# Memory recall of a whole segment in sixteen 32 by 32 tiles, with a new written order that puts all of Q ahead of K

## The chip, the cores and the metric

The kernel runs on one core of one Trainium2 chip. A core has five engines that run side by side and wait for each other only through semaphores: TensorE (PE, matrix products, with PEld for its weight loads), VectorE (DVE), ScalarE (ACT), GpSimd (POOL) and SyncE (SP, whose queue here issues nearly all DMA transfers). Working memory is SBUF, 128 partitions; matrix products land in PSUM, 128 partitions in 8 banks of 512 float32 columns each. The metric is the device time of one execution in microseconds (us); the time of a kernel is the median of its runs. A profile is one execution recorded by the hardware; its span is what lies between its first and last instruction.

## The reference

Two branches over the same input x (2048 tokens by 512) are mixed by a gate per token. Branch A is attention in four segments of 512 tokens with a memory that is carried from segment to segment, 32 heads of 16; branch B is a gated feed-forward layer of width 1792.

```python
for s in range(4):                      # segments of 512 tokens
    logits = einsum('bhqd,bhkd->bhqk', qs, ks) * scale + mask
    a_dot = einsum('bhqk,bhkd->bhqd', softmax(logits), vs)
    pq = phi(qs)                        # where(t > 0, t + 1, exp(t))
    num = einsum('bhld,bhde->bhle', pq, M)
    den = einsum('bhld,bhd->bhl', pq, z)[..., None] + 1e-06
    outs.append(g * num / den + (1 - g) * a_dot)     # g = sigmoid(beta), per head
    M = M + einsum('bhld,bhle->bhde', phi(ks), vs)
    z = z + einsum('bhld->bhd', phi(ks))
a = concat(outs) @ wo
gate, up = x @ W_gate, x @ W_up
b = (relu(gate) * up) @ W_down
g = sigmoid((x * gate_w).sum(-1))
return g * a + (1 - g) * b
```

The product of phi(q) with M is the memory recall; segment 0 has no memory, so recall exists for segments 1, 2 and 3.

## The kernel before

The kernel is first recorded as a list of tasks: each `plan.add` names an engine, a planned duration, what it depends on, the buffers it needs and frees, and a function that emits the instructions. The two strings at the top decide the rest: `ORDER` is the order in which all tasks are emitted, and so the order of each engine's queue, and `UNITS` says which buffer of a ring (or which PSUM bank) each task gets. The planned durations no longer act; they are what a planner used when it wrote the order.

The work of a segment, in chunks c of 128 feature columns (8 heads), one unit u for each chunk of each segment:

- **Start.** x of segment 0 is loaded in rows and transposed by TensorE (L483), with some products on constants ahead to keep TensorE at work (`heat`, L883) and a pair on junk after them (L501). wq comes in four transfers split over the SP and ACT queues, wk in two halves, then wv, the weights of branch B in pieces, and wo in one transfer (`load_cols`, L266). x of later segments comes by a transposing DMA (L273), and again in rows as `xn` (L276) for the token gates.
- **Projections.** `proj_q`, `proj_k` and `proj_v` (matmuls through `full`, L446 where the tile is the whole 128 by 128 array, L450 where it is cut into four column tiles of 32). VectorE copies the results out of PSUM (L542 for Q, L558 for K, L588 for V) and masks K into KT (L561); phi of Q and K is formed with an exponential on ScalarE (L520) and two VectorE instructions (L515, L516). phi(K) is transposed by DMA into pK (L574).
- **Attention.** A visit of scores (`qk`, L609; the diagonal, L622) uses row tiles of 32 by 128: four heads at once, each with its own rows of the array and its own bank of the PSUM banks 0 to 3. ScalarE takes the exponential of four banks at once (L631), GpSimd masks (L660), and `pv` multiplies with V in column tiles of 128 by 32 (L682), twice for each unit, r = 0 and 1. In `pv`, head pair j is written to the PSUM partitions 32j to 32j + 31. `normalise` transposes the result (L713), takes the reciprocal (L721), and scales (L718); L694 transposes it into oT.
- **Memory.** `memory` adds phi(K) times V (L787, column tiles); VectorE accumulates it (L801, L803) and spreads it into `mbd` (L812), a block-diagonal 128 by 128 matrix for each chunk with the head gate folded in through `bdg`, and into `zbd` (L807) for the denominators.
- **Denominators.** `dens` (L738) forms den for two chunks at once; VectorE adds 1e-6, takes the reciprocal (L751) and multiplies with the token ratio (L752); SP stores the result to DRAM as `coefs` (L756).
- **Recall.** `recall` runs once for each chunk of segments 1 to 3, twelve times. SP loads the coefficients, broadcast over partitions, into one of two buffers `cdr` (L765); one plain product of mbd with phi(Q) of 512 columns goes into one bank; VectorE multiplies the bank with the coefficients into `omr` (L773), and L698 adds it to oT.
- **Branch B and output.** `ffn_tasks`: gate and up products, ReLU on ScalarE (L832), the product hT on VectorE (L838); `out_tile` accumulates hT times wd and oT times wo in one bank, VectorE scales (L864) and SP stores (L869).

Whenever two neighbours in TensorE's queue have different tile shapes (plain 128 by 128, row tiles, column tiles), the shape changes between them. Tasks marked `flex` (the plain ones) take the column form when they directly follow a column task.

`head_gates` (L370 to L378) makes the head gates from beta once: four copies (L373) of 32 partitions, four more instructions. Its lines and those of the recall are printed below.

Of the kernel before, what the change touches and what calls it, by code (L numbers as in the profile page):

```python
# [12 lines left out]
P = 128  # L13
S = 2048
D = 512
# [77 lines left out]
"""  # L93

UNITS = (
    "4132650714730167121200005110331202243100000100100000030110000020010300003201100380200103a1"
    "1240231302c02092202211d220b011311361127301512110100201010103223003111212000123231201220000"
    "02300001000003100003200000210003130000000010122b2139220c31140005022a1002022d21103116203802"
    "011027111310011002203223320012310222303120232230310220000022001101000032001121000000301020"
    "1200005000030282125223d11042017023c2231022a11192076412332323020303b01001212203031023111020"  # L100
    "033012131112000002300005000002301112000000230010220000470007242203821000154103102276016222"
    "9406d301b5223417c603a322501001110021"
)


class Slot:


    def __init__(self, cands):
        self.cands, self.units, self.left = tuple(cands), (), 0  # L110

    @property
# [16 lines left out]
class Plan:  # L129
# [18 lines left out]
    def run(self):  # L148
# [7 lines left out]
        for s, n in zip(slots.values(), UNITS):  # L156
            s.units = s.cands[int(n, 16)]
# [21 lines left out]
def kernel(  # L179
# [137 lines left out]
    load_gu(2)  # L317
    load_gu(3)
    got_d = [load_wd(0, 7, "d0"), load_wd(7, NF, "d1")]
    got_o = load_cols(nc.sync, wo_sb, A_wo, 0, D, "o")  # L320
    plan.add("SP", 24500, -1e9, None, xfer=5700.0)


# [563 lines left out]
    for seg in range(NSEG):  # L887
# [15 lines left out]
        for c in range(NC):  # L903
            if seg:
                recall(seg, c)
# [41 lines left out]
```

## Time and profile before

| | us |
|---|---|
| median of 3 runs (266.73 to 267.23) | 266.76 |
| the profiled execution, its own time | 266.88 |
| its span | 265.18 |

The span is 1.6 to 1.7 us shorter than the time, since the time also holds what lies around the first and last instruction. Work of the engines by group, with the costliest of each:

| group | instructions | busy us | mean ns |
|---|---|---|---|
| L446 plain products for gate and up | 393 | 106.8 | 380 |
| L631 exponentials of the scores, ScalarE | 64 | 120.2 | 1878 |
| L838 hT, VectorE | 56 | 38.1 | 685 |
| L713 transposition of the attention result, VectorE | 32 | 22.1 | 703 |
| L773 recall times coefficients, VectorE | 12 | 8.2 | 680 |

Reading it: a matmul's duration (380 ns for 512 columns) runs from its start to its last result, and the next one starts before that, so busy time and the distance between starts are two things. "Idle before" an engine's instruction counts only if that engine is on the chain that ends last.

### The profile page before, as it was taken

The page shows a single profiled execution, that of the slowest core. Times are in us where ns is not written, and L with a number is a line of the kernel's source. Part 1 is how long each engine was busy: PE and PEld are TensorE (multiplying, and loading weights), DVE is VectorE, ACT ScalarE, POOL GpSimd, SP SyncE. Part 2 cuts the span into 40 slices and gives each one's busy share as a digit, 9 for nine tenths or more (in the row PEclk, how much of TensorE's full clock was granted, in tenths as well). Part 3 has the DMA queues.
Part 4 walks back from the last instruction along what each step waited for, and adds up shares of the span by engine and source line. Part 5 has one row for each costly group of instructions (what it writes and reads, how often), then busy time and mean ns, then how long its engine had stood idle before and what let it go on. Part 6 is the DMA issues. An engine that isn't in the chain of part 4 may idle for free.

```text
span 265.2 us, 8154 instructions
## 1 busy us (share of the span) xinstructions
PE 257.7 (97%) x3499; PEld 119.7 (45%) x3530; DVE 202.7 (76%) x456; ACT 182.4 (69%) x168; POOL 60.3 (23%) x162
## 2 busy tenths in 40 slices
PE   8999999999999999999999999999999999999995
PEld 5443444444444344444443444444444544444554
DVE  3497797999997897998967779979777537764822
ACT  3189899879877789888686976984886656841100
POOL 7014262303142043112312141131204040220000
PEclk9999999999999999999999999999999999999999
DMA  7999990030064024252000632500110000300011
GB/s 203 305 256 339 285 165 0 9 96 2 2 125 54 0 76 67 62 92 64 0 2 4 90 75 79 114 4 2 55 38 0 22 2 22 109 0 2 2 62 40
DMA packets 29931, 19.41 MB, mean 73 GB/s; under 512 B 14920, under 2 KB 28360, under 8 KB 29896
## 3 DMA queue, kind: packets, MB, share of 16 engines
q1 hardware_dynamic: 29320, 18.38, 29.7%
q8 instruction: 27, 0.44, 0.7%
q10 hardware_dynamic: 576, 0.52, 0.6%
q14 instruction: 8, 0.07, 0.1%
HBM read 13.21 MB, written 2.55 MB: 59 GB/s over the span
## 4 chain that ended last, share of the span: by engine, by line
PE 94%; DMA 3%; issue 1%; DVE 1%; DVEq 0%
PE ps L446 65%; PE ps L450 12%; PE ps L609 8%; PE ps L682 7%; DMA wk_sb<-in_A_wk_dram 2%; DMA xn<-in_A_x_dram 1%; PE ps L622 1%; PE ps L787 1%; DVE T L713 1%; PE ps L738 0%; DVE osr L864 0%; DVEq L713 0%
## 5 line engine op out<-in xcount | busy, mean ns | idle before, releaser
L631 ACT ACTIVATE E<-ps 128x2048 bf16<-128x2048 f32 x64 | 120.2, 1878 | 30.9 <-PE ps L609 29.2
L660 POOL TENSOR_SCALAR_AFFINE_SELECT E<-E 128x256 bf16<-128x256 bf16 x128 | 52.4, 441 | 171.8 <-ACT E L631 171.8
L838 DVE TENSOR_TENSOR hT<-ps,rgr 128x512 bf16<-128x512 f32 x56 | 38.1, 685 | 23.4 <-PE ps L446 15.8
L446 PE MATMUL ps<-xT,wg_sb 128*128 128x512 bf16 x203 | 55.5, 379 | 0.5 <-issue 0.2
L446 PE MATMUL ps<-xT,wu_sb 128*128 128x512 bf16 x190 | 51.3, 380 | 1.1 <-issue 1.0
L832 ACT ACTIVATE rgr<-ps 128x512 bf16<-128x512 f32 x56 | 32.3, 598 | 19.2 <-PE ps L446 19.0
L446 PE MATMUL ps<-wd_sb,hT 128*128 128x512 bf16 (+1 forms) x163 | 38.6, 352 | 0.6 <-issue 0.5
L446 PEld LDWEIGHTS <-wg_sb 128*128 128x128 bf16 x208 | 19.4, 98 | 23.7 <-issue 2.1
L446 PEld LDWEIGHTS <-wu_sb 128*128 128x128 bf16 x202 | 18.1, 98 | 22.7 <-issue 3.4
L609 PE MATMUL ps<-QT,KT 32*128 32x320 bf16 (+3 forms) x512 | 25.4, 273 | 0.0
L713 DVE STREAM_TRANSPOSE T<-ps 128x512 f32<-128x512 f32 x32 | 22.1, 703 | 4.0 <-PE ps L682 3.7
L446 PEld LDWEIGHTS <-hT 128*128 128x128 bf16 x167 | 14.4, 98 | 16.0 <-issue 2.1
L864 DVE TENSOR_SCALAR osr<-ps,ngcol 128x512 bf16<-128x512 f32 (+2 forms) x18 | 12.3, 687 | 10.2 <-PE ps L450 6.1
L682 PE MATMUL ps<-E,Vp 128*17 128x320 bf16 (+3 forms) x512 | 19.2, 273 | 0.5 <-DVE T L713 0.4
L450 PE MATMUL ps<-wd_sb,hT 128*32 128x512 bf16 (+1 forms) x340 | 19.4, 362 | 0.0
L609 PEld LDWEIGHTS <-KT 32*128 32x128 bf16 x512 | 7.6, 92 | 25.3 <-issue 25.0
L446 PE MATMUL ps<-xT,wq_sb 128*128 128x512 bf16 (+1 forms) x70 | 17.8, 360 | 0.2 <-issue 0.2
L631 ACT ACTIVATE Em<-ps 128x2048 bf16<-128x2048 f32 x8 | 15.0, 1877 | 4.2 <-PE ps L622 4.2
L446 PE MATMUL ps<-xT,wk_sb 128*128 128x512 bf16 x54 | 15.1, 380 | 0.5 <-DMA wk_sb<-in_A_wk_dram 0.2
L558 DVE CAST ktr<-ps 128x512 bf16<-128x512 f32 x16 | 10.9, 686 | 4.8 <-PE ps L446 4.6
L446 PE MATMUL ps<-wv_sb,xT 128*128 128x512 bf16 x46 | 13.2, 380 | 0.3 <-issue 0.2
L446 PE MATMUL ps<-wo_sb,oT 128*128 128x512 bf16 (+1 forms) x54 | 13.2, 356 | 0.1
(97 smaller groups left out, 284.9 us busy)
## 6 DMA issues: line engine op xcount, KB each, us to landing
cdr<-coefs SPq DMA_DIRECT2D x12, 256.0 KB
out_dram<-osr SPq DMA_DIRECT2D x15, 128.0 KB
wd_sb<-in_B_W_down_dram SPq DMA_DIRECT2D x2, 896.0 KB
xn<-in_A_x_dram SPq DMA_DIRECT2D x3, 512.0 KB
wg_sb<-in_B_W_gate_dram SPq DMA_DIRECT2D x2, 512.0 KB
wu_sb<-in_B_W_up_dram SPq DMA_DIRECT2D x2, 512.0 KB
wg_sb<-in_B_W_gate_dram SPq DMA_DIRECT2D x2, 384.0 KB
wu_sb<-in_B_W_up_dram SPq DMA_DIRECT2D x2, 384.0 KB
```

What stands on the lines that cost most here:

```text
L446: nc.tensor.matmul(out, lhsT=lhsT, rhs=rhs, start=start, stop=stop)
L450: nc.tensor.matmul(out[r], lhsT=lhsT[:, r], rhs=rhs, start=start, stop=stop, tile_position=(0, 32 * j))
L558: d = plan.add("DVE", 600, key - RQK, lambda: nc.vector.tensor_copy(ktr[ks.i][:], bank(sl)), [a], DVL + 40, need=[ks], frees=[sl])
L609: nc.tensor.matmul(ps[:, j * L + o:j * L + o + L - q], lhsT=KT[i][rows, kb, 3 * r:3 * r + 2].rearrange("p h q -> p (h q)"), rhs=QT[i][rows ...
L622: nc.tensor.matmul(ps[:, o:o + HP], lhsT=KT[i][rows, kb, 2:4].rearrange("p h q -> p (h q)"), rhs=QT[i][rows, kb * P:kb * P + HP], start=Tr ...
L631: last_exp[0] = [plan.add("ACT", 66 + 4 * L / 1.2, key, lambda: nc.scalar.activation(dst, ps[:, 0:4 * L], ACT.Exp, scale=SCALE), [a] + war ...
L660: nc.gpsimd.affine_select(out=m[:, :, o:o + HP], in_=m[:, :, o:o + HP], compare_op=ALU.is_ge, fill=0.0, base=HP, pattern=[[0, 4], [1, HP]] ...
L682: nc.tensor.matmul(bank(sl)[32 * j:32 * j + HW, q:q + w], lhsT=(Vp[i] if n < 4 else Vm)[:, kb, r, 4 * c + j, 0:HW], rhs=rhs, start=(n == 0 ...
L713: done.append(plan.add("DVE", 633, key - RL, lambda r=r, sl=sl: nc.vector.transpose(T[ts.i][:, r], bank(sl)), [a] + done, 75 if r else 0, ...
L832: r = plan.add("ACT", 478, key - RL, lambda sl=gsl, rs=rs: nc.scalar.activation(rgr[rs.i][:], bank(sl), ACT.Relu), [g], ACL, frees=[gsl])
L838: nc.vector.tensor_tensor(hT[hs1.i][:], bank(sl), rgr[rs.i][:], ALU.mult)),
L864: nc.vector.tensor_scalar(osr[os.i][:, n0 - c0:n1 - c0], bank(sl)[:, 0:n1 - n0], ngcol[:, tt:tt + 1], None, ALU.mult)),
```

## The change

Five edits belong together, and the order is written anew over all of them (1,339 tasks in place of 1,348).

1. **Recall by segment.** `recall(seg)` is one task for a whole segment: for each chunk c and each head pair j, one product of a 32 by 32 tile, at rows 32j and columns 32m of the array with m = (j - c) mod 4, 16 products of 512 columns. Chunk c still has its own bank, so four banks are held at once; the four tiles of one bank come from four different row groups, and the four tiles of one row group go to four banks. Four VectorE multiplications follow, one for each bank.
2. **Rotated partitions.** So that recall and attention line up, head pair j of chunk c now stands at the PSUM partitions 32m in `pv` too. The rows of `wo` are loaded rotated to match, in seven transfers in place of one, and the head gates are rotated: `head_gates` has 25 small VectorE instructions in place of 8, and the mask `bd` is built with copies on GpSimd.
3. **Smaller memory matrix.** `mbd` keeps only its diagonal blocks, 32 columns for each chunk, so that each of the two spreading instructions writes 128 by 64 elements in place of 128 by 256.
4. **Coefficient buffers.** Chunks 0 and 1 use two fixed buffers `cdr`; chunks 2 and 3 use the space of `xn` once the token gates of that segment are formed. The reload of `xn` for the next segment waits for the recall's multiplications of chunks 2 and 3. `omr` has four buffers in place of three.
5. **A new written order**, made with assumed landing times of wq 0.6 us earlier. At the start TensorE's queue has the products of Q chunks 1, 3, 0 (and half of the last) ahead of the first of K; before, the first halves of three K chunks stood between them, and the pair on junk stood ahead of the first Q and now stands between K products. The transposing load of x for segment 2 now stands on SP right behind the first weights. The head gates stand on VectorE before the first feed-forward products are done, in place of after the first segment's first unit.

```diff
-    got_o = load_cols(nc.sync, wo_sb, A_wo, 0, D, "o")
-    plan.add("SP", 24500, -1e9, None, xfer=5700.0)
+    for c in range(NC):
+        n = P - 32 * c
+        nc.sync.dma_start(out=wo_sb[0:n, c, :], in_=A_wo[(c + 1) * P - n:(c + 1) * P, :])
+        if c:
+            nc.sync.dma_start(out=wo_sb[n:P, c, :], in_=A_wo[c * P:(c + 1) * P - n, :])
+    got_o = arrival("o")
+    plan.add("SP", 27500, -1e9, None, xfer=5700.0)
...
+    def turned(c):
+
+        return [(j, (j - c) % 4) for j in range(4)]
+
     def head_gates():
-        gb = gcat[:, 1]
-        for j in range(4):
-            nc.vector.tensor_copy(ebq[32 * j:32 * j + 32], eb.rearrange(
-                "p (c j r) -> p j c r", j=4, r=2)[32 * j:32 * j + 32, j])
-        nc.vector.tensor_scalar(gb, ebq[:], 1.0, None, ALU.add)
-        nc.vector.reciprocal(gb, gb)
-        nc.vector.tensor_tensor(gcat[:, 0], ebq[:], gb, ALU.mult)
-        nc.vector.tensor_tensor(bdg[:], bd.rearrange("p c (j r) -> p c j r", r=2),
-                                gb[:, :, None, :].to_broadcast([P, NC, 4, 2]), ALU.mult)
+        nc.vector.tensor_scalar(gall[:, 1], eb[:], 1.0, None, ALU.add)
+        nc.vector.reciprocal(gall[:, 1], gall[:, 1])
+        nc.vector.tensor_tensor(gall[:, 0], eb[:], gall[:, 1], ALU.mult)
+        g = gall.rearrange("p k (c j r) -> p k c j r", j=4, r=2)
+        for m in range(4):
+            rows = slice(32 * m, 32 * m + 32)
+            nc.vector.tensor_copy(gcat[rows, 1], g[rows, 1, :, m])
+            for c in range(NC):
+                nc.vector.tensor_copy(gcat[rows, 0, c], g[rows, 0, c, (m + c) % 4])
+        for r, m in enumerate((mcol_e, mcol_o)):
+            nc.vector.tensor_scalar(bdg[:, :, r], gcat[:, 1, :, r], m[:, 0:1], None, ALU.mult)
...
-                    for j in range(4):
+                    for j, m in turned(c):
...
-                            bank(sl)[32 * j:32 * j + HW, q:q + w],
+                            bank(sl)[32 * m:32 * m + HW, q:q + w],
...
-    def recall(seg, c):
...
-        a = plan.add("PE", 216, key, lambda col: full(
-            bank(sl), mbd[i][:, c].rearrange("p j r e -> p (j r e)"), pqT[u % RQ][:], True, True,
-            col), [prj["pq", seg, c], att["mbd", seg - 1], (b, 3900.25)], PEL, need=[sl], flex=1)
...
+    def recall(seg):
+        i, sls = seg % 2, [work() for _ in range(NC)]
...
+        coef = [cdr[0][:], cdr[1][:]] + [xn.bitcast(F32).rearrange(
+            "p (k t) d -> p k (t d)", k=2)[:, k] for k in range(2)]
...
+        def pe():
+            for c in range(NC):
+                for j, m in turned(c):
+                    rows = slice(32 * j, 32 * j + 32)
+                    nc.tensor.matmul(bank(sls[c])[32 * m:32 * m + 32],
+                                     lhsT=mbd[i][rows, c].rearrange("p r e -> p (r e)"),
+                                     rhs=pqT[units[c] % RQ][rows, :], start=True, stop=True,
+                                     tile_position=(32 * j, 32 * m))
+        a = plan.add("PE", 230, key, pe, [prj["pq", seg, c] for c in range(NC)]
+                     + [att["mbd", seg - 1]] + [(b, 3900.25) for b in loads], PEL, need=sls,
+                     mode="quad", size=16)
+        for c, u in enumerate(units):
+            om = plan.one("omr")
+            att["recall", u] = a
+            att["omul", seg, c] = plan.add("DVE", 605, key - RL, lambda c=c, om=om: (
+                nc.vector.tensor_tensor(omr[om.i][:], bank(sls[c]), coef[c], ALU.mult)),
+                [a, loads[c]], DVL, need=[om], frees=[sls[c]])
+            recalled[u] = att["omul", seg, c], om
...
-                    mbd[n][:, :, :, r, :],
-                    mzacc[:, :, r, None, 0:DH].to_broadcast([P, NC, 4, DH]),
-                    bdg[:, :, :, r, None].to_broadcast([P, NC, 4, DH]), ALU.mult)
+                    mbd[n][:, :, r, :], mzacc[:, :, r, 0:DH],
+                    bdg[:, :, r, None].to_broadcast([P, NC, DH]), ALU.mult)
...
             got_n[seg] = [plan.add("SP", 520, KA(4 * seg - 4), lambda seg=seg: load_xn(seg),
-                                   att["xn", seg - 1], 6500, xfer=1700.0)]
+                                   att["xn", seg - 1] + [att[k] for k in (
+                                       ("omul", seg - 1, 2), ("omul", seg - 1, 3)) if k in att],
+                                   6500, xfer=1700.0)]
```

More of the change, by code (lines that the diff above doesn't have):

```diff
@@ L30 @@
 ORDER = """
[62 rows of a table removed]
[62 rows of a table added]
 """
 UNITS = (
[L96 to L102, printed above, removed]
+    "765432100132020000013101220024300002310000001000000012000000000300010000320000101003220101"
+    "1333037221411293125003a1206013d023c0128200b00110010001000003000101111202000012221300456102"
+    "1000000300000002300000000200000000021000212021042231103832220016112b200332370109023d102522"
+    "6c010a100010003030007050103121103020013433212012450011000003200000002300000000210002000001"
+    "00022313012212031271013301542062134310a1029420b0218202c113d1100001030206070303030202331200"
+    "004563201000003200000003200000000010000000760000134203022222121201602230025023a504c3137312"
+    "83119407b625d00110112100"
 )
@@ L156, in run @@
         for s, n in zip(slots.values(), UNITS):
-            s.units = s.cands[int(n, 16)]
+            s.units = s.cands[int(n, 36)]
         for t in self.tasks:
@@ L232 @@
     oT = [sb([P, NC, L], BF16, f"oT{i}") for i in range(2)]
-    mbd = [sb([P, NC, 4, 2, DH], BF16, f"mbd{i}") for i in range(2)]
+    mbd = [sb([P, NC, 2, DH], BF16, f"mbd{i}") for i in range(2)]
     zbd = [sb([P, NC, 4, 8], BF16, f"zbd{i}") for i in range(2)]
@@ L243 @@
     cfr = ring([P, 2, 16], F32, "cfr", 2)
-    omr = ring([P, L], BF16, "omr", 3)
+    omr = ring([P, L], BF16, "omr", 4)
     dnr = ring([P, P], F32, "dnr", 2)
-    cdr = ring([P, L], F32, "cdr", 2)
+    cdr = [sb([P, L], F32, f"cdr{i}") for i in range(2)]
     osr = ring([P, D], BF16, "osr", 3)
@@ L255, in work @@
         return plan.one("ps", range(7, -1, -1))
-    LANDS = dict(n0=3600, n1=3800, n2=4300, n3=4450, qa=5700, qb=6450, ka=7250, kb=8550, v=10050,
+    LANDS = dict(n0=3600, n1=3800, n2=4300, n3=4450, qa=5100, qb=5900, ka=7250, kb=8550, v=10050,
                  g0=11550, u0=13000, gw=14400, be=14650, g1=15900, u1=17250, x1=20700, g2=22000,
-                 u2=23100, g3=24200, u3=25300, d0=28100, d1=30800, o=32100)
+                 u2=23100, g3=24200, u3=25300, d0=28100, d1=30800, o=33600)
     def arrival(name):
@@ L334 @@
     bd = sb([P, NC, 8], F32, "bd")
-    nc.gpsimd.memset(bd[:], 1.0)
-    nc.gpsimd.affine_select(out=bd[:], in_=bd[:], compare_op=ALU.is_ge, fill=0.0, base=0,
-                            pattern=[[0, NC], [-16, 8]], channel_multiplier=1)
-    nc.gpsimd.affine_select(out=bd[:], in_=bd[:], compare_op=ALU.is_ge, fill=0.0, base=15,
-                            pattern=[[0, NC], [16, 8]], channel_multiplier=-1)
-    bdg = sb([P, NC, 4, 2], F32, "bdg")
+    bdg = sb([P, NC, 2], F32, "bdg")
     tri = sb([P, P // 2], BF16, "tri")
@@ L350 @@
         nc.gpsimd.memset(zbd[i][:], 0.0)
+    nc.gpsimd.memset(bd[:, 0], 1.0)
+    nc.gpsimd.affine_select(out=bd[:, 0], in_=bd[:, 0], compare_op=ALU.is_ge, fill=0.0, base=0,
+                            pattern=[[-16, 8]], channel_multiplier=1)
+    nc.gpsimd.affine_select(out=bd[:, 0], in_=bd[:, 0], compare_op=ALU.is_ge, fill=0.0, base=15,
+                            pattern=[[16, 8]], channel_multiplier=-1)
+    for g in range(1, NC):
+        nc.gpsimd.tensor_copy(bd[:, g, 0:8 - 2 * g], bd[:, 0, 2 * g:8])
+        nc.gpsimd.tensor_copy(bd[:, g, 8 - 2 * g:8], bd[:, 0, 0:2 * g])
     eb = sb([P, H], F32, "eb")
-    ebq = sb([P, NC, 2], F32, "ebq")
+    gall = sb([P, 2, H], F32, "gall")
     gcat = sb([P, 2, NC, 2], F32, "gcat")
@@ L368 @@
     nc.gpsimd.memset(rcol[:], 0.0)
+    def turned(c):
+        return [(j, (j - c) % 4) for j in range(4)]
     def head_gates():
-        gb = gcat[:, 1]
-        for j in range(4):
-            nc.vector.tensor_copy(ebq[32 * j:32 * j + 32], eb.rearrange(
-                "p (c j r) -> p j c r", j=4, r=2)[32 * j:32 * j + 32, j])
-        nc.vector.tensor_scalar(gb, ebq[:], 1.0, None, ALU.add)
-        nc.vector.reciprocal(gb, gb)
-        nc.vector.tensor_tensor(gcat[:, 0], ebq[:], gb, ALU.mult)
-        nc.vector.tensor_tensor(bdg[:], bd.rearrange("p c (j r) -> p c j r", r=2),
-                                gb[:, :, None, :].to_broadcast([P, NC, 4, 2]), ALU.mult)
+        nc.vector.tensor_scalar(gall[:, 1], eb[:], 1.0, None, ALU.add)
[9 more added lines that the diff above has]
+            nc.vector.tensor_scalar(bdg[:, :, r], gcat[:, 1, :, r], m[:, 0:1], None, ALU.mult)
     got_eb = plan.add("ACT", 200, 0.0, lambda: nc.scalar.activation(
         eb[:], betab[:], ACT.Exp, scale=-1.0), [got_be], 100)
-    got_gates = plan.add("DVE", 1400, 0.0, head_gates, [got_eb], 100, lock=True)
+    got_gates = plan.add("DVE", 2000, 0.0, head_gates, [got_eb], 100, lock=True)
     PEL, DVL, ACL, POL = 230, 150, 165, 130
@@ L682, in pv @@
                         nc.tensor.matmul(
-                            bank(sl)[32 * j:32 * j + HW, q:q + w],
+                            bank(sl)[32 * m:32 * m + HW, q:q + w],
                             lhsT=(Vp[i] if n < 4 else Vm)[:, kb, r, 4 * c + j, 0:HW],
-                            rhs=rhs, start=(n == 0), stop=(n == 7), tile_position=(0, 32 * j))
+                            rhs=rhs, start=(n == 0), stop=(n == 7), tile_position=(0, 32 * m))
             a = plan.add("PE", 550, key - PVP + r, pv, masks + [prj["v", seg, t] for t in range(4)]
@@ L758, in dens @@
             xfer=700.0)
-    def recall(seg, c):
-        i, u, sl = seg % 2, 4 * seg + c, work()
-        key = KA(u - LEAD, -4000)
-        cs, om = plan.one("cdr"), plan.one("omr")
-        n, k = 2 * seg + c // 2, c % 2
-        b = plan.add("SP", 620, key - 3000, lambda: nc.sync.dma_start(
-            out=cdr[cs.i][:], in_=coefs[n][8 * k:8 * k + 8].rearrange("h t p -> h (t p)")[:, None]
-            .to_broadcast([8, 16, L])), [att["coefs", seg, c // 2]], 4200, need=[cs],
-            xfer=1850.0)
-        a = plan.add("PE", 216, key, lambda col: full(
-            bank(sl), mbd[i][:, c].rearrange("p j r e -> p (j r e)"), pqT[u % RQ][:], True, True,
-            col), [prj["pq", seg, c], att["mbd", seg - 1], (b, 3900.25)], PEL, need=[sl], flex=1)
-        att["recall", u] = a
-        a = plan.add("DVE", 605, key - RL, lambda: nc.vector.tensor_tensor(
-            omr[om.i][:], bank(sl), cdr[cs.i][:], ALU.mult), [a, b], DVL, need=[om],
-            frees=[sl, cs])
-        recalled[u] = a, om
+    def recall(seg):
+        i, sls = seg % 2, [work() for _ in range(NC)]
+        key = KA(4 * seg - LEAD, -4000)
+        units = [4 * seg + c for c in range(NC)]
+        coef = [cdr[0][:], cdr[1][:]] + [xn.bitcast(F32).rearrange(
+            "p (k t) d -> p k (t d)", k=2)[:, k] for k in range(2)]
+        loads = []
+        for c in range(NC):
+            n, k = 2 * seg + c // 2, c % 2
+            war = att["xn", seg] if c > 1 else [att.get(("omul", seg - 1, c))]
+            loads.append(plan.add("SP", 620, key - 3000, lambda c=c, n=n, k=k: nc.sync.dma_start(
+                out=coef[c], in_=coefs[n][8 * k:8 * k + 8].rearrange("h t p -> h (t p)")[:, None]
+                .to_broadcast([8, 16, L])), [att["coefs", seg, c // 2]] + war, 4200, xfer=1850.0))
+        def pe():
+            for c in range(NC):
+                for j, m in turned(c):
[14 more added lines that the diff above has]
+            recalled[u] = att["omul", seg, c], om
@@ L819, in memory @@
         a = plan.add("DVE", 290, key, total, [a], 40, frees=[sl])
-        att["mbd", seg] = plan.add("DVE", 900, key, spread, [a] + war, DVL, lock=True)
+        att["mbd", seg] = plan.add("DVE", 620, key, spread, [a] + war, DVL, lock=True)
     def ffn_tasks(seg):
@@ L903 @@
         for c in range(NC):
-            if seg:
-                recall(seg, c)
+            if seg and c == 0:
+                recall(seg)
             attention(seg, c)
```

124 rows, old and new, of the table ORDER are left out of this document.

## The prediction

> **What bounds the kernel now.** I read the first page, then the chain of waits in order of time, then the costliest groups with shapes kept apart, then the stretches of the first 60 us. The page's first part has TensorE busy nearly throughout (the granted clock is 1.00 in the stretches shown further down):
>
> ```profile
> PE 257.7 (97%) x3499; PEld 119.7 (45%) x3530; DVE 202.7 (76%) x456; ACT 182.4 (69%) x168; POOL 60.3 (23%) x162
> ```
>
> The chain in order of time (start, length, what) gives the two prices on which the sum rests:
>
> ```profile
> 72.48 2.70 PE ps L446 x12
> ...
> 124.39 0.73 DVE T L713
> ...
> 139.39 0.73 DVE T L713
> ...
> 144.69 3.13 PE ps L446 x14
> ```
>
> Stretches of 12 and 14 plain matmuls last 2.70 and 3.13 us, so one more costs 0.215, and 2.70 - 12 x 0.215 leaves 0.12 at the end of a stretch: the drain when the tile shape changes. And only in two places does the chain leave TensorE after the start: the second attention-times-V product (L682) of a unit waits for the transposition (L713) of the first, because the old order gives both the same PSUM bank. The timeline of TensorE shows what that costs:
>
> ```profile
> 124.51 0.60 PE L450 MATMUL ps<-xT,wk_sb 128*32 128x512 bf16 x8
> 125.16 0.62 PE L682 MATMUL ps<-E,Vp 128*17 128x448 bf16 x16
> ...
> 138.73 1.04 PE L450 MATMUL ps<-wd_sb,hT 128*32 128x512 bf16 x16
> 140.16 0.62 PE L682 MATMUL ps<-E,Vp 128*17 128x448 bf16 x16 [0.40 <-DVE T L713]
> ```
>
> Column tiles run four at a time, so 8 of them end 2 x 0.215 after their start: the next could begin at 124.94 and begins at 125.16; 16 of them leave it at 139.59 against 140.16. Together 0.79 us. All other waits of TensorE after the first scores (15.6 us) are under 0.1. So time follows the matmuls, the changes of shape, and those waits.
>
> **The change, part by part.** The sum is made against the profiled execution's span, 265.18; the median shown, 266.76, lies 1.58 above it.
>
> *Recall.* Removed are 12 products of 0.215 (10 plain, as the first row has them, and two as four column tiles, L450):
>
> ```profile
> L446 PE MATMUL ps<-pqT,mbd 128*128 128x512 bf16 x10 | 3.8, 381 | 0.1
> ...
> L787 PE MATMUL ps<-Vp,pK 128*32 128x34 bf16 x192 | 2.0, 183 | 0.0
> ```
>
> That is -2.58. Added are three groups of 16 tiles, 32 by 32, 512 columns each. No row shows 16 at once. Floor: all together, 0.215. Ceiling: the four of a bank one after another, 0.86. Nearest are the rows of four tiles, which do overlap, so I take full overlap plus issue: the update of the memory issues 64 small matmuls in 0.70 us, one lasting 0.183 (L787), so 0.52/63 = 8 ns a step; 15 x 8 ns + 0.215 = 0.34. Three: +1.02.
>
> [...]
>
> *Changes of shape.* Counting along both written orders, matmuls change between plain, row, column and 32 by 32 tiles 146 times before and 151 times after: six for entering and leaving the three groups, one fewer elsewhere. 5 x 0.12 = +0.60, bounds 0.5 to 0.7.
>
> *The two waits.* In the new order no unit's two products share a bank (before: those two units). -0.79; at worst the wait comes back elsewhere, 0.
>
> *New small waits.* I take +0.5, bounds 0 to 1.3. After the third recall VectorE must do four products with the coefficients, two transpositions, three additions and the rest before the last output tiles may start; adding these up, it reaches the third addition about 0.2 after TensorE asks. And the head gates: 8 small VectorE instructions become 25, moved from 36 us to about 18 us. Nearest to a copy of theirs are a small MEMSET and the old copies (starts, and the time from first to last):
>
> ```profile
> 1.08 0.35 DVE L332 MEMSET mcol_e<- 16x1 f32 x4
> ```
>
> ```profile
> L373 DVE COPY ebq<-eb x4: 152/162/371, 35.8 to 36.3; 32x8 f32<-32x8 f32 x4
> ...
> ```
>
> The old ones took 1.7 us. Twenty copies at 0.09 (L332, 0.35 for four) to 0.17 (L373, three steps from 35.8 to 36.3) and 0.9 for the other five make 2.7 to 4.3. Queued behind are a ReLU-gated product hT and the next bank's release; by my addition TensorE asks for that bank 0.4 to 0.5 us after VectorE has it at the lower price, and waits 1.0 at the upper. I take 0.3. Later VectorE gets 1.2 back (six L812 of 0.45 shrink fourfold in width; L749 at 128x128 lasts 0.288), but that is covered.
>
> *Start.* All of Q ahead of K removes the gap at 7.93, but the second half of wk lands only at 9.19:
>
> ```profile
> 7.93 0.98 PEld L446 LDWEIGHTS <-wk_sb 128*128 128x128 bf16 x6 [0.53 <-DMA wk_sb<-in_A_wk_dram]
> 9.19 0.57 PEld L446 LDWEIGHTS <-wk_sb 128*128 128x128 bf16 x4 [0.29 <-DMA wk_sb<-in_A_wk_dram]
> ```
>
> The old order has three first halves of K to do meanwhile; the new one runs three Qs to about 8.6 (its first ones still at the slow pitch of the cold start), one first half to 9.0, then waits, and the keep-warm pair sits in the hole before the first score. Same total work, same holes: 0, bounds -0.4 to +0.4. The first score moves from 15.6 to some 11.5, which only shifts work that TensorE does anyway.
>
> *DMA.* wo comes in seven transfers instead of one; at 0.5 us each on SP (its other loads) that is 1 us more than its 2.44, ahead of the second xT, xn and three pK on the same queue. Before, the xT issue holds SP for 4.44 and xn, issued at 33.94, has landed by 38.6; so xn should land near 26.1 + 4.4 + 4.7 = 35.2 for its first reader at about 37, and pK is read by the memory at about 52: covered; without cover, 1 us. xn now holds coefficients of chunks 2 and 3, so its reload queues behind the recall's products. It stands 35 us and 20 us of matmuls ahead of the denominators that need it: 0. Recall needs all four coefficient loads at once, and everything on TensorE queues behind it; before, a coefs store issued at 221.40 had its two loads landed by 230, and with 1.5 of vector work ahead of it (L749, L751, L752) that is 10 us, while the new order has 39, 28 and 14 us of matmuls from the last denominators to the recall: 0, and what is left over at the third is 4. Rotating PV's tiles moves no instruction.
>
> **Sum:** 265.18 - 2.58 + 1.02 + 0.60 - 0.79 + 0.5 = 263.93; with 1.58 around it, 265.5. Its own range, from the bounds above: 264.4 to 266.8, most of it 264.7 to 266.2.
>
> **Rivals.**
>
> *VectorE becomes the bound early (slower).* The new order packs attention of the first segment tighter. These stretches are of before (busy by engine; DVE is the third number pair):
>
> ```profile
> 10.00:20.00 10.00, 9.89 (x61) 4.45 (x61) 9.78 (x24) 6.77 (x8) 0.89 (x2) 1.00 1.07 284
> 20.00:30.00 10.00, 9.84 (x94) 4.04 (x94) 6.99 (x16) 9.08 (x10) 2.97 (x6) 1.00 1.08 342
> 30.00:40.00 10.00, 9.95 (x142) 4.45 (x142) 9.54 (x31) 9.15 (x11) 5.81 (x22) 1.00 1.27 177
> ```
>
> VectorE is busy 44.0 of the 50 us from 10 to 60. Counting the instructions that each order places there, at the means of their rows, gives 48.4 before and 55.5 after (head gates at 3.3); scaled alike (means overlap), 50.4 of 50. If it can hold only the 0.91 it holds from 30 to 60 before, it needs 55.4: 5.4 late, of which some 3 (four gate sums of the next segment and the like) may lag without harm. TensorE then waits 2.4 more: 267.9. It decides once such waits pass 1.3 (no gain). For it: hardly any slack. Against: 9.78 of 10 is held from 10 to 20 while TensorE is 9.89 busy.
>
> *Banks refuse to share.* Each recall group costs 0.86, not 0.34: +1.56, 267.0, no measurable change. For it: no row shows several row tiles in one bank. Against: column tiles already share a bank (L450, L682), and row tiles already run together (L609, each in a bank of its own). A tenth, since no row tests it while each neighbouring one overlaps. [...]
>
> *Waits vanish and none come* (within my range): 264.7.
>
> **Chances.** Forecast with its neighbours 0.60, VectorE bound 0.25, banks 0.10, anything else 0.05. 0.2% of the median, 0.53 us, is about what a measurement of this kernel can tell from no change: faster means below 266.2, slower above 267.3. From the forecast 0.56 falls to faster, 0.04 to same; banks go to same but for tails; VectorE nearly all to slower: 0.57, 0.15, 0.28. For 8 in 10 the range runs from 264.3 to 268.3.
>
> **What would show it.** Right: the tile group's 16 matmuls start within 0.15 us and the next stretch begins 0.45 after the first; no L713 in the chain between 100 and 150 us; first score near 11.5; TensorE's waits for VectorE under 0.2 each between 18 and 60 us. Wrong: four bunches of starts 0.2 apart in the group (banks); waits of L446 for hT or L542 early, with VectorE above 9.7 of 10 (VectorE bound); a recall that waits for its loads.

## The result and the profile after

The changed kernel takes 267.89 us (median of 22 runs, 267.13 to 269.8); the kernel before, run beside it, 267.19 (22 runs, 266.72 to 269.03). The ratio is 1.0035, with a 95% interval of 1.0019 to 1.0051: slower by 0.2 to 0.5%, where 265.5 was predicted. The profiled execution has a span of 266.79 (268.72 with what lies around it), 1.61 above the span before.

TensorE's busy time in the page's first part has hardly moved; the instructions have:

```profile
PE 258.2 (97%) x3647; PEld 120.2 (45%) x3677; DVE 204.2 (77%) x473; ACT 182.3 (68%) x168; POOL 63.7 (24%) x168
```

The chain of waits in order of time shows where the order is no longer held by TensorE:

```profile
6.19 5.80 PE ps L460 x24
...
21.26 0.33 DVE gcat L391 x4
...
122.22 0.36 PE ps L792 x16
122.58 5.30 PE ps L460 x22
127.90 0.69 DVE ktr L572
...
140.13 0.70 DVE ktr L572
140.88 0.73 PE ps L696 x32
```

The two waits for a transposition between 100 and 150 us are gone. In their place the chain runs through VectorE twice: from 16.5 to 25.8 us (the line at 21.26 is part of the head gates) and from 127.9 to 140.9, where it ends in a wait of TensorE. Each recall is a piece of 0.36. And the first line is odd: 24 products, most of them half as wide as usual, in 5.80 us. The timeline of TensorE has the reason beside it:

```profile
3.57 1.91 PE L497 MATMUL ps<-ident,xn 128*128 128x128 bf16 x16
6.19 4.92 PE L460 MATMUL ps<-xT,wq_sb 128*128 128x256 bf16 x20 [0.71 <-DMA wq_sb<-in_A_wq_dram]
10.96 1.46 PE L460 MATMUL ps<-xT,wk_sb 128*128 128x512 bf16 x6
```

TensorE has nothing to do from 5.48 to 6.19, and then its products start 0.213 us apart at 256 columns (0.427 at 512) until 10.2, twice the usual distance (0.109 and 0.216 behind it). In the kernel before, this half pitch ended at 6.3.

So that many small waits can be compared, the table gives **lost time**: the start of a TensorE instruction less the sum of all that stands ahead of it in TensorE's queue, each at its measured distance (0.2157 for 512 columns, 0.10 to 0.14 for a change of shape). It starts near zero; a rise between two rows is a wait between those places. The columns to the right belong to the experiments.

| place (us) | before | after | after again | xn early | + plain wd | all edits |
|---|---|---|---|---|---|---|
| first scores (11 to 16) | -0.1 | 2.0 | -0.1 | 0.4 | -0.3 | 0.1 |
| 33 to 38 | -0.1 | 2.5 | 0.4 | 0.8 | 0.2 | 0.1 |
| 44 to 50 | -0.1 | 2.5 | 1.6 | 0.9 | 0.2 | 0.1 |
| 67 to 72 | -0.1 | 2.7 | 2.1 | 1.0 | 0.3 | 0.3 |
| 84 to 90 | -0.1 | 2.8 | 2.6 | 1.6 | 0.3 | 0.2 |
| 155 to 158 | 0.8 | 3.3 | 3.1 | 2.1 | 0.7 | 0.5 |
| last matmul | 0.6 | 3.5 | 3.4 | 2.4 | 1.0 | 0.8 |
| span | 265.2 | 266.8 | 266.6 | 265.6 | 264.4 | 264.2 |

Span less lost time is 264.6 before and 263.3 after: the work itself is 1.3 shorter, as it should be. 2.9 of new lost time ate it.

### The profile page after: what moved, and what is told of

Its sections match the earlier page's. It is cut to its first block, busy times and chain, and to the rows that moved or that the text cites. A ratio compares the mean times of both kernels' runs of the same rounds, so it can differ in the third digit from the quotient of the medians.

```text
span 266.8 us, 8499 instructions
## 1 busy us (share of the span) xinstructions
PE 258.2 (97%) x3647; PEld 120.2 (45%) x3677; DVE 204.2 (77%) x473; ACT 182.3 (68%) x168; POOL 63.7 (24%) x168
## 4 chain that ended last, share of the span: by engine, by line
PE 86%; DVE 8%; issue 3%; DMA 2%; SPq 0%; ACT 0%; DVEq 0%; ACTq 0%
PE ps L460 53%; PE ps L464 16%; PE ps L623 7%; PE ps L696 7%; DVE junk L414 2%; DMA wq_sb<-in_A_wq_dram 2%; DVE ktr L572 1%; DVE hT L866 1%; DVE KT L575 1%; PE ps L636 1%; PE ps L816 1%; DVE gcat L391 1%; DVE Vp L602 0%; PE ps L792 0%; PE ps L752 0%
## 5 line engine op out<-in xcount | busy, mean ns | idle before, releaser
L674 POOL TENSOR_SCALAR_AFFINE_SELECT E<-E 128x256 bf16<-128x256 bf16 x128 | 53.9, 445 | 171.0 <-ACT E L645 171.0
L460 PE MATMUL ps<-xT,wg_sb 128*128 128x512 bf16 x179 | 50.3, 380 | 0.6 <-issue 0.3
L460 PE MATMUL ps<-xT,wu_sb 128*128 128x512 bf16 x165 | 45.9, 380 | 0.4 <-issue 0.2
L460 PE MATMUL ps<-wd_sb,hT 128*128 128x512 bf16 (+2 forms) x168 | 37.5, 344 | 0.5 <-issue 0.5
L460 PEld LDWEIGHTS <-wg_sb 128*128 128x128 bf16 x186 | 17.1, 98 | 21.7 <-issue 3.0
L460 PEld LDWEIGHTS <-wu_sb 128*128 128x128 bf16 x170 | 15.4, 98 | 19.4 <-issue 2.8
L460 PEld LDWEIGHTS <-hT 128*128 128x128 bf16 x174 | 15.4, 98 | 16.0 <-issue 1.5
L464 PE MATMUL ps<-wd_sb,hT 128*32 128x512 bf16 x312 | 20.5, 379 | 0.0
L460 PE MATMUL ps<-xT,wq_sb 128*128 128x512 bf16 (+1 forms) x64 | 17.0, 394 | 0.9 <-DMA wq_sb<-in_A_wq_dram 0.7
L460 PE MATMUL ps<-xT,wk_sb 128*128 128x512 bf16 x58 | 16.9, 379 | 0.3 <-issue 0.2
L460 PE MATMUL ps<-wv_sb,xT 128*128 128x512 bf16 x54 | 15.8, 380 | 0.6 <-issue 0.6
L464 PE MATMUL ps<-xT,wu_sb 128*32 128x512 bf16 x216 | 14.3, 379 | 0.0
```

Source lines behind the costliest of these rows:

```text
L460: nc.tensor.matmul(out, lhsT=lhsT, rhs=rhs, start=start, stop=stop)
L464: nc.tensor.matmul(out[r], lhsT=lhsT[:, r], rhs=rhs, start=start, stop=stop, tile_position=(0, 32 * j))
L674: nc.gpsimd.affine_select(out=m[:, :, o:o + HP], in_=m[:, :, o:o + HP], compare_op=ALU.is_ge, fill=0.0, base=HP, pattern=[[0, 4], [1, HP]] ...
```

## The experiments

Four theories were held against each other. Theory 1: the start (TensorE idle ahead of wq, then half pitch) costs the time. Theory 2: VectorE falls behind after 18 us, the prediction's slower rival. Theory 3, formed after the first four runs: the load of xn for the second segment pins the order at 41 us. Theory 4, formed after eight, an inference from when a stop comes: TensorE runs out of instructions at 82 us. All runs had the kernel before run beside them; the ratios are to it.

### The start

`e1` is the changed kernel again. `e2` moves the pair on junk back:

```diff
 ORDER
-... 31 30 34 35 32 63 36 76 ... 55 67 56 37 68 ...
+... 31 30 34 35 32 37 63 36 76 ... 55 67 56 68 ...
```

`e3` does that with five products in place of two:

```diff
-                    for h in range(2):
+                    for h in (0, 1, 0, 1, 0):
```

and `e4` moves the pair the other way in the kernel before (`... 9 78 37 68 ...` in its order).

> The changed kernel once more, unaltered, for a second profile and more times. Theory 1 (the start): in the first profile TensorE stood still from 5.48 to 6.19 us, waiting for wq, and its products then ran at half pitch (0.213 us for 256 columns) until 10.2; whether the half pitch lasts that long changes from run to run. It expects a median near 267.9 with a spread of 2 us or more, and in the profile either the same 4 us of half pitch (span 266 to 267) or half pitch that ends near 6.5 (span near 264.9). Theory 2 (VectorE falls behind after 18 us, the rival of the prediction): the loss is the same in each run, so a spread under 1 us, and waits of TensorE for VectorE of 2 us in all between 18 and 60 us.

> The changed kernel with the pair of products on junk back ahead of the first product of Q (into a bank that is free there); nothing else moved. Theory 1: TensorE has work from 5.3 to 5.7 and waits at most 0.5 for wq; if that is enough, half pitch ends near 6.5 and the median falls by 1 to 1.7, to 266.2 to 266.9; if the 0.5 that is left still spoils it, the time stays near 267.9. Theory 2: within 0.3 of the changed kernel (267.6 to 268.2).

> As the run with the pair first, but with five products on junk in place of two, 1.07 us at half pitch: TensorE is busy without a break from the first transposition to 6.5 us, past the landing of wq. Theory 1: half pitch always ends by 6.7, the spread falls under 1 us, the first product of Q starts at about 6.4 and the median is 266.0 to 266.6. Theory 2: within 0.3 of 267.9, or later by up to 0.4.

> The kernel before, with the pair of products on junk moved from ahead of the first product of Q to between the products of K, where the changed kernel has it; nothing else. Theory 1: if wq lands after 5.5 here too, TensorE stands still ahead of the first Q in many runs, half pitch lasts to about 10 in those, and the median rises by 0.5 to 1.7 over the kernel before (267.7 to 268.9) with a wider spread. Theory 2: 0 to 0.4 faster than before, since the pair does nothing useful.

| | median (n) | range | before | ratio |
|---|---|---|---|---|
| e1 | 268.17 (12) | 267.07 to 269.67 | 267.10 (35) | 1.0029 [1.0011, 1.0047] |
| e2 | 268.02 (12) | 267.14 to 268.92 | 267.10 | 1.0029 [1.0014, 1.0043] |
| e3 | 267.84 (12) | 267.46 to 269.62 | 267.10 | 1.0032 [1.0016, 1.0048] |
| e4 | 267.45 (12) | 266.60 to 268.34 | 267.10 | 1.0007 [0.9994, 1.0020] |

The profile of e1 settles more than the times. Its half pitch ended at 4.1, and the first scores start at 11.47 in place of 13.62: the quick start that I had forecast. Yet its span is 266.6 against 266.8. The 2.1 us of the start were given back later, 1.15 of them between 33 and 45 us (table). e2 and e3 have quick starts too, and end at 266.4 and 266.1. In e4 wq lands late (first Q at 6.00), 0.55 is lost at the first scores, and the time can't be told from the kernel before. Theory 1 falls as the cause: what a quick start gains is lost at a place that has a fixed time of its own. Theory 2's numbers came true in part (e2 and e3 within 0.3 of the changed kernel and about 2 us of waits for VectorE in e1, but no spread under 1 us), and 1.15 of the 2 us have another origin. VectorE's timeline in e1 shows it:

```profile
36.76 0.65 DVE L866 TENSOR_TENSOR hT<-ps,rgr 128x512 bf16<-128x512 f32 x1
38.77 0.86 DVE L414 SCALAR_TENSOR_TENSOR junk<-xn,gwb 128x512 bf16<-128x512 bf16 x1 [1.36 <-DMA xn<-in_A_x_dram]
...
40.28 0.69 DVE L572 CAST ktr<-ps 128x512 bf16<-128x512 f32 x1
```

VectorE stands still for 1.36 us with the first token gate of the next segment, whose rows have not landed. Behind the second token gate in the same queue comes the copy of K out of its bank, and TensorE waits for the bank (TensorE's timeline of e1):

```profile
41.02 1.05 PE L464 MATMUL ps<-xT,wu_sb 128*32 128x512 bf16 x16 [0.95 <-DVE ktr L572]
```

In e2 and e3 that token gate starts at 38.64 and 38.51, again after a wait for the load. In the first profile of the changed kernel VectorE came to it only at 39.39 and waited for nothing: there the slow start hid the late load.

```profile
39.39 0.67 DVE L414 SCALAR_TENSOR_TENSOR junk<-xn,gwb 128x512 bf16<-128x512 bf16 x1
```

### The load of xn

```diff
-    for c in range(NC):
-        n = P - 32 * c
...
+    def load_wo():
+        for c in range(NC):
+            n = P - 32 * c
...
-    plan.add("SP", 27500, -1e9, None, xfer=5700.0)
+    plan.add("SP", 27500, -1e9, load_wo, xfer=5700.0)
 ORDER
-... 22 26 670 23 27 ... 239 339 145 ...
+... 22 26 27 ... 239 339 23 670 145 ...
```

(339 loads xn, 23 wo, 670 xT for segment 2.)

> The changed kernel with one edit: on SP's queue the load of xn for the second segment stands ahead of the seven loads of wo and of the load of xT for segment 2, in place of behind them. In the profiles with a quick start, VectorE waits for this load from 37.4 to 38.8 us and TensorE then 1.1 us for VectorE at 41 us. Theory 3 (the load of xn pins the order at 41 us, so that a quick start is lost there): that wait goes, the quick-start profiles have about 0.5 us of lost TensorE time by 43 us in place of 1.6, and the median falls by 0.7 to 1.1 from 268.0 to 266.9 to 267.3. Theory 2 (VectorE alone cannot keep up with the new order before 60 us): TensorE's waits for VectorE come back within 10 us, and the median stays within 0.3 of 268.0.

267.37 (12 runs, 266.77 to 268.65), ratio 1.0017 [1.0002, 1.0033]. (Lines of this kernel and of those built on it are two or more higher: L460 is L462.) The wait at 41 is gone in TensorE's timeline, and from 31 to 60 us no new one comes (column "xn early"):

```profile
39.74 0.61 PE L698 MATMUL ps<-E,Vp 128*17 128x448 bf16 x16
40.18 0.29 PE L698 MATMUL ps<-Em,Vm 128*17 128x64 bf16 x16
40.30 1.04 PE L466 MATMUL ps<-xT,wu_sb 128*32 128x512 bf16 x16
```

The times agree in direction (0.5 under the first 22 runs of the changed kernel, 0.8 under e1), but their spreads overlap, so the size of the gain rests on the traces. There theory 3 holds, and theory 2 loses its main claim. SP's queue in e1 shows why the load was late:

```profile
28.48 0.32 SPq L324 DMA_DIRECT2D wo_sb<-in_A_wo_dram  x1
31.86 1.86 SPq L273 DMA_TRANSPOSE xT<-in_A_x_dram  x1
33.85 0.49 SPq L276 DMA_DIRECT2D xn<-in_A_x_dram  x1
```

The wo loads hold the queue from 23.21 to 28.80. The issue of xT starts 3.1 later; the list of SP's waits puts 3.0 of it down to the transfer of wd, which stands ahead in the queue (2.7 in the first profile). The load of xn, issued at 33.85, releases VectorE at 38.7.

### The head gates later

`e6` alone, `e7` with xn early and the pair first, `e8` as e7 and with the copy of K (719) ahead of masks at 140 us:

```diff
 ORDER of e6, e7, e8
-... 213 25 214 ... 240 49 147 ...
+... 213 214 ... 240 25 49 147 ...
 ORDER of e8
-... 625 737 734 718 736 675 638 753 626 676 801 719 800 ...
+... 625 737 718 753 719 734 736 675 638 626 676 801 800 ...
```

> The changed kernel with one edit: the 25 small VectorE instructions of the head gates (18.3 to 21.6 us, 3.3 us) moved back to just ahead of the first instruction that reads them (L450, 31 us). Theory 3: TensorE's waits of 0.2 and 0.1 us between 22 and 31 us go, but the wait for xn at 41 takes them up: within 0.3 of 268.0. Theory 2: the gates are what VectorE lacks early; the waits up to 31 us (0.45) go and the median falls by 0.3 to 0.5.

> The changed kernel with three edits together: xn early, head gates late, and the pair of products on junk ahead of the first Q. Theory 3: the sum of the parts, lost TensorE time by 43 us of 0.2 or less in place of 1.5 to 2.5, median 266.4 to 266.8, faster than the kernel before (267.1). Theory 2: 267.4 to 268.0, with the lost time found again between 31 and 60 us.

> As the run with the start mended, and on VectorE the copy of K out of its bank (L572, at 140.1 us) stands ahead of three masks of K and the clamp of the token gates (L575 twice, L575, L418), with the second copy of Vm ahead of it. In the changed kernel TensorE waits 0.5 us there for the bank. Theory 3, for which the rest of the loss is single waits on VectorE's order: 0.4 to 0.5 less than the run with the start mended, 266.0 to 266.4. Theory 2: less than 0.2 of difference, the wait moves on.

270.32 (ratio 1.0124 [1.0105, 1.0143]), 270.31 (1.0125 [1.0104, 1.0147]) and 270.60 (1.0131 [1.0112, 1.0150]), of 4 to 5 runs each: e6 and e7 lie 2 us above the most that either theory gave them (268.3 and 268.0). The 0.45 up to 31 us did go, but TensorE's timeline of e6 has this:

```profile
35.31 0.59 PE L460 MATMUL ps<-wv_sb,xT 128*128 128x512 bf16 x2 [2.07 <-DVE QT L556]
```

The copy of Q out of its bank stands three instructions behind the gates on VectorE. 3.3 us of gates moved in ahead of it, and 2.1 of them came out as a wait of TensorE: VectorE had little more than 1 us to spare at 31 us. So theory 2 has a part of the truth. The order leaves VectorE little room for late work, though it can keep up where no load stops it.

By the scores at 38 TensorE had lost 3.1 in e6, and 0.9 of that is half pitch, not waiting: just behind the stop the granted clock fell to 0.50, from 36.2 to 39.6 us (in e7 from 37.1 to 40.5). The fall is not what makes these kernels slow. In e8's profile TensorE stops as long (2.1) with a mean clock of 0.999, and two runs of e6 with a mean clock of 1.000 took 270.21 and 270.86.

In e8 the loss at 140 us fell only from 0.49 to 0.33, and TensorE now waits there for a transposition (L729): the wait moved on, as theory 2 expected.

### The stop at 82 us

In all but one (e3) of the profiles of the new order so far, TensorE stops at one and the same instruction, at 82 to 86 us. TensorE's timeline of e1:

```profile
83.31 0.39 PE L464 MATMUL ps<-wd_sb,hT 128*32 128x512 bf16 x4
84.16 1.05 PE L464 MATMUL ps<-wd_sb,hT 128*32 128x512 bf16 x16 [0.46 <-issue]
```

No engine is named, only "issue". Of 0.84 between the two starts, 0.215 is usual. The page's part on DMA queues lists 28 packets of kind "instruction", 0.46 MB, so 16 KB each, and the trace says when each ran:

| | transfer (us) | TensorE restarts | stop beyond 0.215 |
|---|---|---|---|
| e3 | 81.12 to 82.18 | (83.38) | 0 |
| after | 81.93 to 83.19 | 84.32 | 0.18 |
| e2 | 81.31 to 82.57 | 83.91 | 0.47 |
| e1 | 81.26 to 82.69 | 84.16 | 0.62 |
| e5 | 80.25 to 81.88 | 83.15 | 0.67 |
| e6 | 82.71 to 84.13 | 85.60 | 0.67 |
| e8 | 82.97 to 84.60 | 86.05 | 0.93 |
| e7 | 83.49 to 85.20 | 86.62 | 1.07 |
| e11 (below) | 80.91 to 82.63 | 84.17 | 1.09 |

Each transfer begins about 240 recorded TensorE instructions ahead of the stop, and TensorE restarts 1.1 to 1.5 us after it ends. Just there the new order puts the memory update (64 small products), denominators, scores, a product with V and 48 column tiles of wd next to each other. The shape of these tiles alone is not the cause: in e3, whose transfer ended 1.2 us ahead, the same tiles ran on without a stop. `e9` is e5 with the wd products plain (315 is the first of the seven tasks, and the others follow its shape):

```diff
-                t.col = bool(t.flex) and mode == "col"
+                t.col = bool(t.flex) and mode == "col" and t.n != 315
```

> The run with xn early, and the seven tasks of hT times wd that follow the product with V at 82 us are written as plain products in place of column tiles (12 matmuls in place of 48, with their weight loads). Theory 4 (TensorE runs out of instructions there): in seven of the eight profiles so far TensorE stands still 0.1 to 1.1 us too long at the same instruction, some 235 recorded instructions after the start of a transfer of 16,384 bytes on the queue for instructions, whenever that transfer ends less than about 1.5 us ahead. It expects that the stop of 0.6 us at 82 to 84 us goes, less 0.1 for one more change of shape, and a median 0.3 to 0.5 below the run with xn early (266.9 to 267.1). Theory 2 (it is VectorE that is late there too): the stop stays, and the time is within 0.15 of 267.4 or 0.1 above it.

266.59 (9 runs, 265.94 to 267.73), ratio 0.9978 [0.9963, 0.9994], 0.8 under e5 (theory 4 had 0.3 to 0.5) and now faster than before. TensorE's timeline of e9 at the place:

```profile
81.46 0.29 PE L698 MATMUL ps<-Em,Vm 128*17 128x64 bf16 x16
81.68 2.76 PE L462 MATMUL ps<-wd_sb,hT 128*128 128x512 bf16 x11
```

The stop is gone. Two things speak for theory 4: 12 matmuls in place of 48 took the stop away, and in eight profiles TensorE restarted 1.1 to 1.5 us after the end of the transfer. That instructions were missing meanwhile is an inference, since the profile names no releaser. Of the 0.8, 0.6 is the stop; the rest lies within the spread of the two medians. The two profiles differ by 1.3 (spans 265.63 and 264.36), since e9's also happened to start quicker: first scores at 11.28 against 11.96.

### Banks in turn

```diff
-            for c in range(NC):
-                for j, m in turned(c):
+            for j in range(4):
+                for c in range(NC):
+                    m = (j - c) % 4
```

> The changed kernel with the 16 tiles of each recall group issued by row group (four banks in turn) in place of bank by bank (four row groups into one bank, one after another); same products. If row tiles that share a bank cost nothing, the group lasts the same 0.36 to 0.37 us from its first start to the next stretch. If they wait for each other in some part, it is shorter here, 0.30 to 0.33.

TensorE's timeline of the changed kernel, then of this run:

```profile
122.14 0.43 PE L792 MATMUL ps<-pqT,mbd 32*32 32x512 bf16 x16
122.51 0.60 PE L460 MATMUL ps<-xT,wg_sb 128*128 128x512 bf16 x2
```

```profile
122.00 0.43 PE L793 MATMUL ps<-pqT,mbd 32*32 32x512 bf16 x16
122.37 0.60 PE L460 MATMUL ps<-xT,wg_sb 128*128 128x512 bf16 x2
```

0.37 in both (e11 has a single execution, 268.67). That the order makes no difference would not settle it alone, since the same four tiles share each bank in both; what does is that 16 tiles are through in 0.37, where four of 0.215 one after another would take 0.86. Row tiles that share a bank, each with other partitions of it, do not wait for each other in this kernel.

### All edits, and the pair alone

`e10` is e9 with the pair first, the copy of K first, and the rotated half of the head gates in 7 strided copies in place of 16:

```diff
-            for c in range(NC):
-                nc.vector.tensor_copy(gcat[rows, 0, c], g[rows, 0, c, (m + c) % 4])
+            for c0, c1 in ((0, 4 - m), (4 - m, 4)):
+                if c1 > c0:
+                    q = 5 * c0 + m - (4 if c0 else 0)
+                    nc.vector.tensor_copy(gcat[rows, 0, c0:c1], gall[rows, 0].rearrange(
+                        "p (q r) -> p q r", r=2)[:, q:q + 5 * (c1 - c0) - 4:5])
```

`e12` is e9 with the pair first alone (the edit of e2).

> All that helped together: xn early, plain products of wd at 82 us, the pair on junk ahead of the first Q, the copy of K ahead of the masks at 140 us, and the rotated half of the head gates copied in 7 strided instructions in place of 16 (same result, 16 instructions in place of 25). Theory 3 with 4: lost TensorE time at the end of 1.2 to 1.5 us in place of 2.35, median 266.2 to 266.7, faster than the kernel before (267.0) by 0.1 to 0.3%. Theory 2: not under 267.0.

> The run with xn early and plain wd, and the pair of products on junk ahead of the first Q; the head gates and the copy of K stay as in the changed kernel. Theory 1, in what is left of it (now that nothing at 41 us swallows a quick start, the slow start shows in the time): the spread shrinks from 1.8 us to under 0.9, with the upper end near 266.7 in place of 267.7, and the median falls by 0.1 to 0.4 from 266.6. Otherwise, where the pair is without effect and the K copy and the shorter head gates made the gain of the run with all edits: median and spread as before it, 266.6 and 1.8.

e10: 265.96 (6 runs, 265.61 to 266.19), ratio 0.9956 [0.9944, 0.9969], the fastest of all, faster than both kernels and a little under the 266.2 that was expected at best. e12: 266.52 (12 runs, 265.87 to 268.00), ratio 0.9971 [0.9954, 0.9988], not to be told from e9. So the pair has no effect that these runs can show. What a late start costs can now be seen, though: e12's profile comes to the first scores 0.71 after e9's (11.99 against 11.28), and its span is 0.82 longer (265.18 against 264.36), since no late load evens it out. What falls of theory 1 is that the pair prevents this. Between e12 and e10 stand the shorter gates and the copy of K, 0.6 together; which gave how much was not taken apart.

## Why the prediction was wrong, step by step

- **Recall: right.** The 16 starts lie within 0.05 us (3.3 ns a step, 8 taken), and the group with the change of shape behind it lasts 0.37. Full overlap plus issue was the right row. The rival of banks that refuse to share falls: the four tiles of a bank write different partitions of it, and one after another they would have made 0.86 of the group.
- **Changes of shape and removed products: near in size.** Predicted -2.58 + 1.02 + 0.60 = -0.96; measured -1.3 (span less lost time). A group with the changes around it took 0.46 (0.37, and 0.09 ahead of it) where the sum has 0.34 and two changes of 0.12; three times 0.12 less is the difference.
- **The two waits: half right.** Both went. One wait of 0.49 came back at 140 us, for the same reason (a bank not yet free), but behind the copy of K that came late, at the end of 13 us in which the chain runs through VectorE.
- **New small waits: the step that failed.** I took 0.5, bounds 0 to 1.3. In the profiles with a quick start TensorE loses 0.5 up to 33 us (head gates; 3.3 us measured, as taken), 1.15 at 41, 0.3 at 50, 0.6 at 82, 0.5 at 140 and 0.4 up to 170: 3.4 in the end against 0.6 before. So there are some 3.4 of new waits (the old ones, 0.79, are gone) where the term has 0.5 and at most 1.3. (The range was also tighter than its own bounds: 1.02, 0.70, no gain from the two waits, 1.3 and 0.4 at the start add up to 267.6, not 266.8.) For the stop at 82 I had no term at all: in the trace of before the longest stop of TensorE with no releaser but "issue" is 0.2. The row to ask was how many TensorE instructions each microsecond of the new order holds.
- **DMA: "covered" was wrong, its price was right.** I put the landing of xn at 35.2 for a reader at 37 and priced the missing cover at 1 us. wo held the queue for 5.6 where I had 3.4, xT began 3.1 after that (3.0 of it a wait for the transfer of wd), and xn landed at 38.7. The reader came at 37.4, and the 1 us (1.15) was due.
- **Start: 0 with bounds of 0.4 was right for the quick starts (first scores near 11.5, as forecast) and wrong for the first profile** (2.05). But it hardly matters for the end of the changed kernel: what the start gained or lost, the late load evened out.
- **The rival "VectorE becomes the bound early"** named 267.9, the time that came; that was luck, since its mechanism is only part of it. One of its signs did show: TensorE waits for hT early (0.2 in the first profile, 0.3 in e1) with VectorE busy 9.78 of 10 from 20 to 30 us. But it held that VectorE could keep no more than 0.91 busy. In e9 the stretches (DVE is the third number pair) show more:

```profile
20.00:30.00 10.00, 9.65 (x160) 4.41 (x163) 9.72 (x35) 9.52 (x10) 5.33 (x17) 1.00 1.09 345
30.00:40.00 10.00, 9.95 (x141) 4.25 (x138) 9.72 (x23) 9.34 (x9) 4.54 (x12) 1.00 0.80 189
```

VectorE is 9.72 of 10 busy and TensorE still 9.65 and 9.95. The time was met by a sum of a load, the stop at 82 and VectorE's order, not by VectorE's capacity.

With the load, the stop and the order mended (e10), the span is 264.2 and the time 265.96, against 263.9 and 265.5 of the sum.

## What to carry to other kernels

When an order is packed tighter, price the loads that its first readers now meet earlier, through the whole queue that issues them, and not only the instructions that change. Two profiles of one kernel that start 2 us apart and end together point to an event with a fixed time between them; find the first wait that the early one has and the late one lacks. And where many small tiles stand next to each other, count instructions as well as columns: here 12 plain products in place of 48 column tiles took away a stop of 0.67.

## What was unexpected in the hardware

- TensorE stopped at 82 to 86 us with no releaser but "issue", for 0.18 to 1.09 us in eight profiles. Transfers of 16 KB on the queue for instructions took 0.9 to 1.7 us, and the stop ended 1.1 to 1.5 us after such a transfer; with 12 plain matmuls in place of 48 column tiles there it was gone.
- TensorE's half pitch at the start ended between 3.7 and 6.4 us in all profiles but the first of the changed kernel (before 6.3, e1 4.1). There TensorE stood still for 0.71 before 6.19, and half pitch ended at 10.2. What sets its end no run shows: e1 has a wait for wq of 0.6 too, and its half pitch was over at 4.1. In e6 and e7, after the stop of 2.1 us, the granted clock fell to 0.50 for 3.41 us; in e8's profile a stop as long had no such fall. The granted clock in the stretches of the profile reads 1.00 during the half pitch at the start and does not show it.
- Sixteen tiles of 32 by 32 with 512 columns start 3.3 ns apart in the changed kernel and run together: the next stretch begins 0.37 after the first start, whether four row groups write one bank in a row or four banks in turn.
